# A two-layer decode kernel: wider copies in the chain's matmuls, another first head in the second layer, and finer V transfers

## The chip, the cores and the metric

The kernel runs on one core of a Trainium2 chip. The metric is the device time of one execution in microseconds (us), and lower is better. A core has a matrix engine (TensorE: PE for its matmuls, PEld for its weight loads), VectorE (DVE), ScalarE (ACT), GpSimd (POOL) and SyncE (SP), which here issues every transfer. Transfers run on 16 DMA engines. Matmul results land in PSUM, which has eight banks of 512 fp32 columns; everything else lies in SBUF.

## The reference

Two layers run one after the other with the same weights and the same caches. Each is an attention block with cached keys and values, and then an MLP block. B = 8 rows (batch), one new token each, D = 448, 16 query heads on 8 cached heads, 4096 cached positions, head size 256, all bf16.

```python
def A(x, k_cache, v_cache, wq, wo):      # x: [8, 1, 448], caches: [8, 8, 4096, 256]
    q = (x @ wq) in 16 heads of 256      # two query heads to a cached head
    p = softmax(q @ k.T * 256 ** -0.5)   # over 4096 positions
    return (p @ v) @ wo
def B_(x, w1, w2, w3, w4):
    h = gelu(layernorm(x) @ w1)          # shifted along S by pads; S = 1, so the shifts leave zeros
    x1 = x + shifted(h) @ w2
    return x1 + gelu(layernorm(x1) @ w3) @ w4
x = x + A(layernorm(x)); x = x + B_(layernorm(x))    # layer 1
x = x + A(layernorm(x)); x = x + B_(layernorm(x))    # layer 2
```

With S = 1 every shifted part is zero, so the w1 and w2 products drop out. What stays is attention, projection, and the w3/w4 MLP. Nearly all bytes are the caches: a head of K or V of one row is 2 MB, or four *quarters* of 512 KB.

## The kernel before, in words

**Slots.** SBUF has 30 slots of one quarter (`kv`). A row needs its K and V in both layers. To read less, some quarters stay in SBUF from the first layer to the second: K of the five *kept* heads 3 to 7 (`KEEP_K`), and six quarters of V (`KEEP_V`: all of head 7, quarters 2 and 3 of head 6). K must be transposed on the way (four fp32 transposes into a bank `psT`, L1145, then a copy back by DVE, L1129, or ACT, L1130). The last two quarters of head 7's K (`HOLD`) don't go back to SBUF at first: they stay transposed in the four `psT` banks until the second layer. Then their place is made by scoring head 7's quarters 0 and 1, after which the banks are copied into those slots (`back_in` in `front`). Heads 0 to 2 are the *free* heads; nothing of them is kept.

**Stages of a row.** `front` takes one head's scores: 16 matmuls a quarter with the cached keys as weights and the query as the moving operand, copied 24 times over two columns, 48 columns in all (L972), then the softmax. `back` does the PV product (8 matmuls a quarter, L1033), sums the four partition groups (L1057) and multiplies by `wo` (L1082). After the eighth head of layer 1 comes what is called the *chain* here: the turn of the summed projection row into columns (10 matmuls) and the last head's projection (20), both on L914 and L917; the norm's sums (L710); 56 matmuls with w3 (L818); gelu; 70 matmuls with w4 (L914, L917, `y_mm`); and the second layer's queries, 16 matmuls a head (L802). All of these have one useful column. It is copied along the moving operand: 24 times for queries and w3 (`QW`, `HW`), 12 times for w4, the turn and the projection (`YW`). Results of the chain and the scores share one PSUM bank, `psM`: scores from column 256 on, the chain's from `SC` = 448 and `YC` = 451 on.

**Order.** The program is written as a list of operations with priorities (`Plan.op`). A planner (`Plan.schedule`) runs them through a model of the engines with fixed durations and puts each engine's instructions in a fixed order; the chip then waits by semaphores, but never reorders. The planner does three things that matter here.
- Loads have a fixed order (`prio=loads[0]`), and SP is in order. `next_kv` joins up to four neighbouring quarters of one head into one transfer if as many neighbouring slots are free. A slot is free when the last PV or score on its old content is done.
- Where PE would idle over 0.1 us, it puts in `filler` matmuls (L1344) as long as the columns in the last 3.413 us are under `TARGET` = 3500. For an operation of the chain it counts 20 columns a matmul, whatever its real width (`pe`).
- The chain's operations have priority over all others (`CH`).

The order of heads in the second layer comes from `MIX` and `l2_heads`: 7, 6, 5, 4, 3, then the free ones 0, 1, 2. While a row's chain runs, the next row's free heads 0 to 2 have their scores already; their `back`, 12 quarters of V, is what the DMA loads then. After these come V of the second layer: head 6 (two quarters), 5, 4, then K of head 0, and so on. `mid` runs the chain's MLP and the queries of the first `QFIRST` heads (`QLAST` in the last row); `fronts_of` takes the queries of the other heads, one head ahead.

Of the kernel before, what the change touches and what calls it, by code (L numbers as in the profile page):

```python
# [8 lines left out]
D = 448  # L9
HKV = 8  # L10
DH = 256
F = 1792
NC5 = 5
# [8 lines left out]
KEEP_V = 6  # L22
# [5 lines left out]
OUT_AT = 23.5  # L28
QLAST = 1
BACKS = (0, 3, 6)  # L30
# [3 lines left out]
PV1 = PV0 + DH  # L34
QW, HW, YW = 24, 24, 12
SC = 448
YC = 451

# [20 lines left out]
class Unit:  # L59

    def __init__(self, tile, u, keep):
        self.tile, self.u, self.keep, self.slot = tile, u, keep, None


class Plan:
# [67 lines left out]
    def schedule(self):  # L135
# [30 lines left out]
        n = 0  # L166
# [14 lines left out]
        def next_kv(i):  # L181

            u = sp_next[i].unit
            m = 1
            while m < 4 and i + m < len(sp_next) and sp_next[i + m].unit is not None and \
                    sp_next[i + m].unit.tile is u.tile and sp_next[i + m].unit.u == u.u + m and \
                    sp_next[i + m].unit.keep == u.keep:
                m += 1  # L190
            late = max(free["sp"], dma_end - self.LEAD)
            times = sorted(set(x for x in self.free_at if x < 1e9))
            if not times:
                return None
            for t in [max(free["sp"], times[0])] + [x for x in times if free["sp"] < x <= late]:
                fit = [(k, a) for k, a in runs(t) if k >= m]
                if fit:
                    break
            else:
                t = max(late, times[0])  # L200
                m = min(m, max(k for k, a in runs(t)))
                fit = [(k, a) for k, a in runs(t) if k >= m]

            before = sp_next[i - 1].unit if i else None
            if before is not None and before.tile is u.tile:
                for k, a in fit:
                    if a <= before.slot + 1 <= a + k - m:
                        return t, m, before.slot + 1
            k = min(k for k, a in fit)
            fit = [a for k2, a in fit if k2 == k]  # L210
            q = min(fit) if u.keep else max(fit) + k - m
            return t, m, q
# [235 lines left out]
def bass_interleave_layers__gqa_block_cached__mixer_s_mlp__decode_kernel(  # L448
# [160 lines left out]

    def load(cache, b, h, units, keep=()):  # L610

        out = {}
        tile = (cache, b, h)
        for u in units:
            x = out[u] = Unit(tile, u, u in keep)
            o = plan.op("sp", None, 0.0, "kv", wr=[("s", x, 0), ("s", x, 1)], prio=loads[0])
            o.unit = x
            loads[0] += 1
        return out
# [45 lines left out]

    CH = -10 ** 6
    urge = [CH]

# [4 lines left out]

    def pe(fn, n, rd=(), wr=(), banks=(), name="chain", prio=None, pairs=None):
        if prio is None:
            prio = urge[0] + len(plan.ops)
        d = 0.06 + 0.026 * n
        return plan.op("pe", fn, (d, d, 20 * n, pairs or n), name, rd=rd, wr=wr, banks=banks, prio=prio)

# [145 lines left out]
    def column_sums():  # L825

        def one(kc):
            return mask[:, kc:kc + 1]
        for g in range(4):
            pe(lambda t, g=g: q_mms(t, range(8 * g, 8 * g + 8), one, psM, SC, 1, QW), 32,  # L830
               rd=["mask"] + WQ, wr=["psM"], banks=[M], prio=len(plan.ops))

            dv(lambda v, g=g: v.tensor_copy(
                cs_q[:, 8 * g:8 * g + 8].rearrange("p (h c j) -> p h c j", c=2, j=2),
                psM[:, SC:SC + 8].rearrange("p (h j c) -> p h c j", c=2, j=2)),
               rd=["psM"], wr=["cs_q"], banks=[M], prio=len(plan.ops))

    def column_sums_h():
        def one(kc):
            return mask[:, kc:kc + 1]  # L840
        pe(lambda t: h_mms(t, one, psM, SC, 1, HW), 56, rd=["mask"] + W3, wr=["psM"], banks=[M],
           prio=len(plan.ops))
        dv(lambda v: v.tensor_copy(cs_h[:, :], psM[:, SC:SC + 14]), rd=["psM"], wr=["cs_h"], banks=[M],
           prio=len(plan.ops))
# [3 lines left out]
    def mlp(src, skey, n, dst, dkeys):  # L848

        few = n < 3  # L850
        ch, kb, bk = (psM[:, SC:], "psM", M) if few else where[0]
        yw, yc = (YW, YC - SC) if few else (n, 0)
        m = 14 * n
        h_, a_, b_ = hb[:, 0:m], g1[:, 0:m], g2[:, 0:m]
        if few:

            sums(src, skey, n)
            moments(True, n)

            for r in range(n):  # L860
                dv(lambda v, r=r: v.tensor_scalar(t_h[:, r * 14:(r + 1) * 14], cs_h[:, :], minus_mean(n, r),
                                                  rsy[:, 1, r:r + 1], ALU.mult, ALU.mult),
                   rd=["mom", "rsy", "cs_h"], wr=["t_h"] if r == 0 else [("t_h", r)])
            pe(lambda t: h_mms(t, lambda kc: src[:, kc, 0:n], ch, 0, n, HW if n == 1 else 12), 56,
               rd=[skey] + W3, wr=[kb], banks=[bk])
            for r in range(n):
                dv(lambda v, r=r: v.scalar_tensor_tensor(
                    hb[:, r:m:n], ch[:, r:m:n], rsy[:, 1, r:r + 1], t_h[:, 14 * r:14 * r + 14],
                    ALU.mult, ALU.add), rd=[kb, "rsy", "t_h"] + [("t_h", r)] * (r > 0),
                   wr=["hb"] if r == 0 else [("hb", r)], banks=[bk])  # L870
        else:
            norm(src, skey, True, n)
            pe(lambda t: h_mms(t, lambda kc: yb[:, kc, 0:n], ch, 0, n, n), 56,
               rd=YB + W3, wr=[kb], banks=[bk])
            dv(lambda v: v.tensor_copy(h_, ch[:, 0:m]), rd=[kb], wr=["hb"], banks=[bk])
# [20 lines left out]
        def y_mm(t):  # L896
# [6 lines left out]
            return last  # L903
        pe(y_mm, 70, rd=["hT"] + W4, wr=[kb], banks=[bk])
        ps4 = ch[:, yc:yc + NC5 * yw].rearrange("p (a n) -> p a n", n=yw)[:, :, 0:n]
# [20 lines left out]
    KEPT_K[HKV - 1] = range(4 - HOLD)  # L926
    KEPT_V = {HKV - 1: range(max(4 - KEEP_V, 0), 4), HKV - 2: range(min(8 - KEEP_V, 4), 4)}
    done = {}

    def front(layer, b, h):  # L930

# [25 lines left out]
        for u in range(4):  # L957
# [6 lines left out]
            def sc(t, u=u, q=ks[u]):  # L964
                last = None
                for s in range(8):
# [9 lines left out]
                    rd=qk + [("s", ks[u], 0), ("s", ks[u], 1)],  # L976
                    wr=[("sc", par, x) for x in range(u, 4)], banks=[bk])
            if u in back_in:
# [34 lines left out]
    def back(layer, b, h):  # L1013
# [10 lines left out]
        fresh_v = [u for u in range(4) if u not in vs]  # L1024
        vs.update(load(A_v_cache, b, h, fresh_v, keep_v))
        for u in range(4):
# [62 lines left out]
        if k == HKV - 1:  # L1089
# [5 lines left out]
            def turn(t):  # L1095
# [6 lines left out]
            pe(turn, 10, rd=["hb", "g1", "g2", "hT", "selR"], wr=["psM"], banks=[M], name="turn",  # L1102
               prio=hi)
            dv(lambda v: v.tensor_tensor(acc[layer][:, :], xin, psM[:, YC:YC + NC5 * YW:YW], ALU.add),
               rd=["psM", xk], wr=[ak], banks=[M], name="acc", prio=hi)
        if k == HKV:
            def wo_mm(t):
# [6 lines left out]
                return last  # L1114
            pe(wo_mm, 20, rd=[("oT", no), "wo0"], wr=["psM"], banks=[M], name="wo", prio=hi)
            dv(lambda v: v.tensor_tensor(xout, acc[layer][:, :], psM[:, YC:YC + NC5 * YW:YW], ALU.add),
# [17 lines left out]
    def transpose_piece(i, pc, hold):  # L1134

        while tcount[0] % NT in held_banks:
            tcount[0] += 1
# [39 lines left out]
    def mid(b, heads):  # L1177

        src = x2c[b % 2]
        mlp(x1c[b % 2], ("x1", b), 1, src[:, :, 0:1], [("x2", b)])  # L1180
        sums(src, ("x2", b), 1, SC + 32)
        second_queries(b, heads[0], None, lambda: dv(
            lambda v: v.tensor_single_scalar(mom2[b % 2][:, :], psM[:, SC + 32:SC + 35], 1.0 / D, ALU.mult),
            rd=["psM"], wr=[("mom2", b)], banks=[M]))
# [12 lines left out]
    def second_queries(b, h, prio, then=lambda: None):  # L1197

        q, src = q2T[b % 2], x2c[b % 2]
        pe(lambda t: q_mms(t, range(4 * h, 4 * h + 4), lambda kc: src[:, kc, 0:1], psM, SC,  # L1200
                           1, QW), 16, rd=[("x2", b)] + WQ, wr=["psM"], banks=[M], prio=prio)
        then()
# [30 lines left out]
    def first_queries():  # L1233
# [14 lines left out]
        for c in range(2):  # L1248
# [3 lines left out]
               dur=0.3, rd=["psM"], wr=[("q1T", c)], banks=[M])  # L1252

    free_heads = list(range(HKV - KEEP_K))
    kept_heads = list(range(HKV - KEEP_K, HKV))
    l2_heads = kept_heads[::-1]

    q_todo = {}

    def fronts_of(layer, b, h):  # L1260
        if layer:

            todo = q_todo[b]
            for h2 in [x for x in todo if x == h] + [x for x in todo if x != h][:1]:
                second_queries(b, h2, len(plan.ops))
                todo.remove(h2)
        front(layer, b, h)

# [4 lines left out]
    def both(layer, b, heads, ahead=(), lag=1):  # L1273
# [4 lines left out]
        for i in range(n + lag):  # L1278
            if i < n:
                tasks.append(("f", layer, b, heads[i]))  # L1280
            tasks += [("f",) + a for a, at in zip(ahead, AT[3 - len(ahead):]) if at == i - n]
            if i >= lag:
# [30 lines left out]
    for b in range(B):  # L1313
# [3 lines left out]
        mid(b, order2[:first])  # L1317
        q_todo[b] = order2[first:]
        if b < B - 1:
            run([("b", 0, b + 1, h) for h in free_heads])  # L1320
# [82 lines left out]
```

## Time and profile before

| | |
|---|---|
| time, median of 4 runs | 1111.84 us (1109.38 to 1116.4) |
| the profiled execution's own time | 1114.11 us |
| its span, first to last instruction | 1112.0 us |
| PE, PEld, DVE, ACT, POOL busy | 87%, 70%, 51%, 26%, 9% |
| mean granted clock of TensorE | 0.931 |
| bytes moved, mean rate | 441.13 MB, 397 GB/s |
| transfers of V | 137 of 512 KB, 49 of 1024, 3 of 1536, 55 of 2048 |
| time from issue to landing (median) | 7.6 us for 512 KB, 16.6 us for 2048 KB |

The profile is one execution. Its span is cut into 40 slices, with busy shares, the clock that TensorE was granted, and the rate of the DMA. Other views list instructions in order of time, who waited for whom, and sums over chosen stretches. A matmul's time is partly modelled, so a busy PE isn't PE at its peak.

### The profile page before, as it was taken

Reading aid. Unit: us, or ns where it says so; the run is one execution under the profiler, and the core shown is the slowest. Engines: PE = TensorE matmul, PEld = TensorE weight load, DVE = VectorE, ACT = ScalarE, POOL = GpSimd, SP = SyncE. Lnnn points to the kernel's source line nnn. Section 1 sums busy time; section 2 is a strip of 40 time slices with the busy share of each in tenths; the row PEclk is TensorE's granted clock in tenths of the full one; section 3 lists DMA queues with packets and bytes.
Section 4 is the critical chain, followed back from the end, with each engine's and each line's share of the span. In section 5 each row is a group of like instructions: output and inputs, shape, how many; then the busy total and the mean of one; then the engine's idle time right before and its main releaser. Section 6 shows DMA issues by size and latency. Waiting matters only on the chain.

```text
span 1112.0 us, 42670 instructions
## 1 busy us (share of the span) xinstructions
PE 965.2 (87%) x19528; PEld 778.9 (70%) x19528; DVE 570.4 (51%) x1784; ACT 286.2 (26%) x841; POOL 97.6 (9%) x275
## 2 busy tenths in 40 slices
PE   5899889897889988898888897988879898898987
PEld 4678657785668756697577775778557785696674
DVE  4345445564455553565445554555445665365544
ACT  1133113340223312243123321233112331233120
POOL 0000010010100101011010100100010000111010
PEclk9899999997999988899899998999899998899897
DMA  9999999999999999999999999999999999999893
GB/s 335 409 425 419 390 403 423 425 416 374 395 426 425 393 340 421 423 426 416 351 423 425 421 378 371 423 423 422 394 384 425 424 399 363 413 424 415 322 419 167
DMA packets 56115, 441.13 MB, mean 397 GB/s; under 512 B 6000, under 2 KB 9216, under 8 KB 28800
## 3 DMA queue, kind: packets, MB, share of 16 engines
q1 hardware_dynamic: 55936, 438.41, 97.0%
q8 instruction: 153, 2.51, 0.9%
q14 instruction: 26, 0.21, 0.0%
HBM read 438.38 MB, written 0.01 MB: 394 GB/s over the span
## 4 chain that ended last, share of the span: by engine, by line
PE 54%; DMA 36%; DVE 5%; issue 3%; SPq 1%; ACT 0%; POOL 0%
DMA kv<-in_A_k_cache_dram 24%; PE psT L1145 20%; PE psM L972 15%; DMA kv<-in_A_v_cache_dram 11%; PE psP L1033 8%; PE psR L1082 3%; PE psM L802 2%; PE psM L914 1%; PE psM L917 1%; DVE oS L1047 1%; PE psP L1057 1%; DVE oS L1049 1%; PE psM L818 1%; SPq L604 1%; PE psP L1344 1%
## 5 line engine op out<-in xcount | busy, mean ns | idle before, releaser
L1145 PE MATMUL psT<-ident_f,kv 128*128 128x128 f32 x2816 | 393.0, 285 | 28.3 <-DMA kv<-in_A_k_cache_dram 25.1
L1129 DVE COPY kv<-psT 128x512 f32<-128x512 f32 x418 | 286.8, 690 | 176.1 <-PE psT L1145 173.2
L1145 PEld LDWEIGHTS psT<-ident_f,kv 128*128 128x128 f32 x2816 | 315.8, 145 | 51.7 <-DMA kv<-in_A_k_cache_dram 31.9
L1130 ACT COPY kv<-psT 128x512 f32<-128x512 f32 x318 | 185.1, 586 | 465.6 <-PE psT L1145 393.8
L1033 PE MATMUL psP<-kv,pT 128*2 128x256 bf16 x4096 | 175.1, 289 | 30.7 <-DMA kv<-in_A_v_cache_dram 16.4
L972 PEld LDWEIGHTS psM<-q2T,kv 128*128 128x128 bf16 x4096 | 124.0, 98 | 49.6 <-issue 40.3
L972 PE MATMUL psM<-q2T,kv 128*128 128x48 bf16 x4096 | 138.8, 186 | 17.4 <-issue 14.7
L972 PEld LDWEIGHTS psM<-q1T,kv 128*128 128x128 bf16 x4096 | 135.8, 97 | 17.7 <-issue 10.9
L972 PE MATMUL psM<-q1T,kv 128*128 128x48 bf16 x4096 | 144.7, 184 | 1.4 <-issue 1.0
L1033 PEld LDWEIGHTS psP<-kv,pT 128*2 128x2 bf16 x4096 | 80.9, 84 | 65.1 <-DMA kv<-in_A_v_cache_dram 21.3
L993 POOL PARTITION_ALL_REDUCE gm<-pm x128 | 45.4, 355 | 753.8 <-DVE pm L991 750.6
L988 DVE COPY sS<-psM 128x64 f32<-128x64 f32 x128 | 28.6, 223 | 132.9 <-PE psM L972 129.5
L1003 ACT ACTIVATE pT<-sS,nb,fac 128x32 bf16<-128x32 f32 x128 | 52.7, 418 | 162.5 <-DVE nb L997 162.5
L1047 DVE CAST oS<-psP 128x256 bf16<-128x256 f32 x128 | 54.0, 422 | 49.6 <-PE psP L1033 47.0
L1082 PE MATMUL psR<-wo_sb,oT 128*1 128x448 bf16 x448 | 68.1, 388 | 7.1 <-DVE oT L1063 3.6
L1007 POOL PARTITION_ALL_REDUCE Db<-rs x128 | 51.0, 398 | 225.3 <-ACT pT L1003 225.3
L1057 PEld LDWEIGHTS psP<-sel,oS 128*128 128x128 bf16 x512 | 25.6, 99 | 52.4 <-DVE oS L1049 46.2
L1057 PE MATMUL psP<-sel,oS 128*128 128x2 bf16 x512 | 32.2, 166 | 33.1 <-DVE oS L1049 32.4
L1003 ACT ACTIVATE pT<-sS,nb 128x32 bf16<-128x32 f32 x128 | 40.9, 326 | 74.3 <-DVE nb L997 74.3
L1049 DVE TENSOR_TENSOR oS<-psP,oS 128x256 bf16<-128x256 f32 x128 | 54.1, 423 | 3.1
L802 PE MATMUL psM<-x2c,wq_sb 128*128 128x24 bf16 x768 | 36.4, 184 | 4.5 <-issue 2.2
L802 PEld LDWEIGHTS psM<-x2c,wq_sb 128*128 128x128 bf16 x768 | 30.2, 98 | 14.2 <-issue 5.6
(156 smaller groups left out, 580.6 us busy)
## 6 DMA issues: line engine op xcount, KB each, us to landing
kv<-in_A_k_cache_dram SPq DMA_DIRECT2D x66, 2048.0 KB, 20.0
kv<-in_A_v_cache_dram SPq DMA_DIRECT2D x55, 2048.0 KB, 16.6
kv<-in_A_v_cache_dram SPq DMA_DIRECT2D x137, 512.0 KB, 7.6
kv<-in_A_v_cache_dram SPq DMA_DIRECT2D x49, 1024.0 KB, 11.1
kv<-in_A_k_cache_dram SPq DMA_DIRECT2D x32, 1024.0 KB, 11.9
kv<-in_A_k_cache_dram SPq DMA_DIRECT2D x4, 1536.0 KB, 11.7
kv<-in_A_k_cache_dram SPq DMA_DIRECT2D x12, 512.0 KB, 7.9
kv<-in_A_v_cache_dram SPq DMA_DIRECT2D x3, 1536.0 KB, 8.3
```

Source lines behind the costliest of these rows:

```text
L802: last = t.matmul(bank[:, at + i * step:at + i * step + copies], w, r, start=(kc == 0), stop=(kc == 3))
L972: last = t.matmul(ps[:, SB + 2 * i:SB + 2 * i + 2 * REP], a[:, c:256:2], bcast(rhs(c), REP, 1), start=(c == 0), stop=(c == 1))
L1003: return a.activation(pT[nr][:, :, :].rearrange("p i j -> p j i")[:, jj, :], sview[:, jj, :], ACT.Exp, bias=nb[nm][:, jj:jj + 1], scale=sc ...
L1007: plan.op("pool", lambda gp: gp.partition_all_reduce(Db[nr][:, :], rs[nr][:, :], P, RO.add), 0.5, "sum", rd=[("rs", nr, 0), ("rs", nr, 1)] ...
L1033: last = t.matmul(ps[g4:g4 + 2, PV0:PV0 + DH], pT[nr][:, i, :], slot_ap(q, s * 256, 256), start=(i < 4), stop=(i >= 28), skip_group_check= ...
L1047: plan.op("dve", lambda v: v.tensor_copy(oS[:, 0, :], po), 0.36, "o", rd=[("pv", par, x) for x in range(4)], wr=["oS0"], banks=[bk], prio=hi)
L1049: plan.op("dve", lambda v: v.tensor_tensor(oS[:, 1, :], po, oS[:, 0, :], ALU.subtract), 0.36, "o", rd=["oS0"] + [("pv", par, x) for x in r ...
L1057: last = t.matmul(ps[:, PV1 + 2 * c:PV1 + 2 * c + 2], oS[:, w, c:DH:2], sel[:, :], start=(w == 0), stop=(w == 1))
L1082: last = t.matmul(psR[r:r + 1, 0:D], oT[no][:, i % 2, i // 2:i // 2 + 1], wo_sb[:, a:a + D], start=(k == 1 and i < 2), stop=(k == HKV - 1 ...
L1129: return e.tensor_copy(dst, psT[bank][:, :])
L1130: return e.copy(dst, psT[bank][:, :])
L1145: last = t.transpose(psT[bank][:, s * P:(s + 1) * P], src, ident_f[:, :])
```

## The change

The matmuls of the chain get 48 copies of their one column instead of 24 or 12 (36 columns' worth for the first MLP product of the last two rows, which has two useful columns). The w4, turn and projection results move to columns 0 to 239 of `psM`, which are zeroed once; the second norm's sums move from `SC` + 32 to `SC` + 56. The planner now counts the chain's real widths, and a longer duration for it where it believes the clock to be low.

The second layer's order of kept heads becomes 6, 7, 5, 4, 3. All four quarters of head 6's K are in SBUF. The queries of a further head follow a `front` instead of going ahead of it, and in the last row the chain takes the queries of two heads.

V of the free heads of every row but the first, in layer 1, is loaded one quarter a transfer.

```diff
-QLAST = 1
+QLAST = 2
+QAFTER = 1
+BOOST = None
+L2 = (3, 4, 2, 1, 0)
+MOST = 1
+MOST2 = 4
-QW, HW, YW = 24, 24, 12
+QW, HW, YW = 48, 48, 48
-YC = 451
+YC = 0
...
-            while m < 4 and i + m < len(sp_next) and sp_next[i + m].unit is not None and \
+            while m < u.most and i + m < len(sp_next) and sp_next[i + m].unit is not None and \
...
-    def pe(fn, n, rd=(), wr=(), banks=(), name="chain", prio=None, pairs=None):
+    def pe(fn, n, rd=(), wr=(), banks=(), name="chain", prio=None, width=20):
         d = 0.06 + 0.026 * n
-        return plan.op("pe", fn, (d, d, 20 * n, pairs or n), name, rd=rd, wr=wr, banks=banks, prio=prio)
+        return plan.op("pe", fn, (d, max(d, 0.06 + n * width / 1200), width * n, n), name, ...)
...
-            pe(lambda t: h_mms(t, lambda kc: src[:, kc, 0:n], ch, 0, n, HW if n == 1 else 12), 56,
+            pe(lambda t: h_mms(t, lambda kc: src[:, kc, 0:n], ch, at, n, HW if n == 1 else 36), 56,
...
-        pe(y_mm, 70, rd=["hT"] + W4, wr=[kb], banks=[bk])
+        pe(y_mm, 70, rd=["hT"] + W4, wr=[kb], banks=[bk], width=yw)
...
-        vs.update(load(A_v_cache, b, h, fresh_v, keep_v))
+        most = MOST if (layer == 0 and b and h in free_heads) else MOST2 if h == l2_heads[1] and layer else 4
+        vs.update(load(A_v_cache, b, h, fresh_v, keep_v, most))
...
-        sums(src, ("x2", b), 1, SC + 32)
+        sums(src, ("x2", b), 1, SC + 56)
...
+        dv(lambda v: v.memset(psM[:, 0:NC5 * YW], 0.0), dur=0.3, rd=[("q1T", 0), ("q1T", 1)],
+           wr=["psM"], banks=[M])
...
-    l2_heads = kept_heads[::-1]
+    l2_heads = [kept_heads[i] for i in L2]
...
     def fronts_of(layer, b, h):
-        if layer:
-            todo = q_todo[b]
-            for h2 in [x for x in todo if x == h] + [x for x in todo if x != h][:1]:
-                second_queries(b, h2, len(plan.ops))
-                todo.remove(h2)
-        front(layer, b, h)
+        if not layer:
+            return front(layer, b, h)
+        todo = q_todo[b]
+        if h in todo:
+            todo.remove(h)
+            second_queries(b, h, len(plan.ops))
+        if not QAFTER and todo:
+            second_queries(b, todo.pop(0), len(plan.ops))
+        front(layer, b, h, BOOST if h == first2[b] else None)
+        if QAFTER and todo:
+            second_queries(b, todo.pop(0), len(plan.ops))
```

`BOOST` = None and `MOST2` = 4 leave priorities and sizes as they are.

## The prediction

> **What bounds the kernel now.** I read the page first: engines, transfer rates, chain.
>
> ```profile
> PE 965.2 (87%) x19528; PEld 778.9 (70%) x19528; DVE 570.4 (51%) x1784; ACT 286.2 (26%) x841; POOL 97.6 (9%) x275
> GB/s 335 409 425 419 390 403 423 425 416 374 395 426 425 393 340 421 423 426 416 351 423 425 421 378 371 423 423 422 394 384 425 424 399 363 413 424 415 322 419 167
> DMA packets 56115, 441.13 MB, mean 397 GB/s; under 512 B 6000, under 2 KB 9216, under 8 KB 28800
> PE 54%; DMA 36%; DVE 5%; issue 3%; SPq 1%; ACT 0%; POOL 0%
> ```
>
> The rate sits at 420 to 426 GB/s and dips eight times. 441.13 MB at 424 GB/s would take 1040 us, so 72 of the 1112 us are not streaming. The last quarter of V lands at 1097.5 us, so 14.5 us are the tail; about 7 us are the start (22.3 MB moved by 60 us). The rest are the dips. Next, the stretches view: two stretches between dips, then 27 us around each dip. Columns: stretch, length, busy time of PE, PEld, DVE, ACT, POOL, then granted clock, DMA share, GB/s.
>
> ```profile
> 170.00:245.00 75.00, 68.70 (x1242) 59.98 (x1235) 44.17 (x108) 27.14 (x74) 6.78 (x18) 0.98 1.00 423
> 707.00:780.00 73.00, 66.63 (x1228) 57.73 (x1226) 42.14 (x103) 25.28 (x68) 6.77 (x18) 0.98 1.01 423
> ```
> ```profile
> 126.00:153.00 27.00, 23.33 (x580) 16.27 (x581) 12.57 (x60) 3.10 (x11) 1.51 (x4) 0.94 1.01 392
> 259.00:286.00 27.00, 21.54 (x520) 14.51 (x523) 12.08 (x58) 2.29 (x7) 0.75 (x2) 0.75 0.95 349
> 393.00:420.00 27.00, 21.55 (x522) 14.76 (x525) 12.15 (x58) 2.19 (x7) 0.75 (x2) 0.80 0.92 337
> 527.00:554.00 27.00, 22.60 (x560) 15.64 (x561) 13.09 (x61) 3.20 (x11) 1.38 (x4) 0.87 0.95 351
> 660.00:687.00 27.00, 22.95 (x560) 16.02 (x558) 13.46 (x61) 2.30 (x7) 1.11 (x3) 0.87 0.96 354
> 792.00:819.00 27.00, 23.35 (x550) 15.85 (x551) 11.95 (x59) 2.30 (x7) 1.11 (x3) 0.81 0.97 359
> 926.00:953.00 27.00, 22.89 (x583) 15.91 (x582) 14.22 (x65) 3.10 (x11) 1.36 (x4) 0.87 0.96 360
> 1027.00:1054.00 27.00, 24.10 (x519) 17.70 (x518) 15.68 (x64) 4.42 (x13) 1.11 (x3) 0.81 0.89 322
> ```
>
> A dip's loss is 27 - 27 x rate/424: 2.0, 4.8, 5.5, 4.6, 4.5, 4.1, 4.1, 6.5, together 36 us. That pot is what the change can reach. Each dip is a row's chain (out projection, MLP, queries). Why it starves the DMA shows in the timeline of the fifth dip (start, length, engine, line):
>
> ```profile
> 670.51 1.27 PE L914 MATMUL psM<-hT,w_sb 128*128 128x12 bf16 x42
> 671.72 1.45 PE L917 MATMUL psM<-hT,w_sb 128*64 128x12 bf16 x28
> 673.10 0.60 PE L1033 MATMUL psP<-kv,pT 128*2 128x256 bf16 x8
> ...
> 676.44 0.80 PE L972 MATMUL psM<-q2T,kv 128*128 128x48 bf16 x16
> 677.28 0.59 ACT L1130 COPY kv<-psT 128x512 f32<-128x512 f32 x1 [7.26 <-PE psM L972]
> 677.53 0.68 DVE L1129 COPY kv<-psT 128x512 f32<-128x512 f32 x1
> ...
> 678.77 0.97 PE L972 MATMUL psM<-q2T,kv 128*128 128x48 bf16 x32
> ```
>
> At a chain 18 K and 6 V quarters are kept, so 6 of the 30 slots circulate. A V quarter landed at 669.62; its PV matmuls stood behind the second MLP product and ran at 673.10; only then did SP issue into that slot (673.74). Twelve V quarters of the next row's free heads go round like this, then V of heads 6, 5, 4. A full round of 6 quarters lasts 6 x 1.25 = 7.5 us and an issue needs 4.0 us at least to land, so 3.5 us of delay on PE are free and the rest is lost.
>
> **48 copies.** Added columns per chain: 56 x 24 = 1344 (first product), 70 x 36 = 2520 (second), 20 x 36 + 10 x 36 = 1080 (projection and turn), 16 x 24 = 384 for each head's queries. Their own time at full clock is nothing: 16 matmuls of 48 columns (L972) take 0.57 us, some 25 ns apart, no more than 16 of 24 columns (L802, 0.61). At half clock the 48-column ones take 0.80, 40 ns apart, while L802 keeps its 0.61 (673.74 to 674.35 us).
>
> What they buy is clock. I added up matmul columns in windows of 3.41 us (the length of the shortest half-clock spell in the clock records; fp32 counted twice, PV a quarter, since four run side by side). Of 29 windows under 2500 columns, 28 are followed by half clock; of 24 between 2500 and 3000, 12; of 259 above, 1. The second dip's windows hold 1836, 1816, 1536, 1820; the third's 2580, 2600, 1064, 2548. Some 5,700 added columns lift most of these over 3000. Against that stand fillers (L1344, 248 columns), which the planner places up to a target of 3500 and will place less often: 102 in the eight stretches, 3,200 columns a dip. Net at least +2,500. Half clock in the stretches is 2 x 27 x (1 - clock), together 69 us; I expect 25, so 44 less. Price: loss against half-clock time over the eight dips gives 0.28 us per us; without the first, where weights still land, 0.13. So 6 to 12 us; I take 8, nearer the lower slope, since the chain's own latency does not shrink. A ceiling: PV of a quarter takes 0.60 against 0.39 us, scores 0.80 against 0.57, some five such pieces a window, 13 windows, 13 us. The floor is below zero: see the last rival.
>
> The Trainium skill (TensorE: Matmul & The Clock Gate, HAM oscillation) gives as the rule that PE must have no idle gap above about 3.4 us. The longest PE idle in the fifth stretch is 1.57 us, yet its clock is 0.87. By the rule alone there would be nothing to win here and this term would be 0; the rows decide against it.
>
> **Head 6 first.** Head 7's quarters 2 and 3 lie in the transpose banks; after its first score two evictions (0.59 and 0.68 us) must pass, and its four scores last 3.35 us on average from first to last over the eight rows, freeing two slots; head 6's four slots follow until 6 to 9 us. Head 6 first: 64 scores at 27 ns are 1.8 us, four slots by about 2.3 us, head 7's two some 3 us later; and only one head's queries stand before the first score (16 matmuls, 0.55 us less). So V of heads 5 and 4 is issued 1 to 2 us earlier. It pays only where landings after the first score are starved: 0.9 to 1.8 us in the second and fifth dip, under 0.5 in others. Between 0 and 8 us in all, I take 4. Two queries in the last row's chain and the later query of the next head: 16 matmuls moved, hidden by PV, 0 (0.5 us if uncovered). The 240-column memset: 0.27 us by the 256-column row, once, under the first loads.
>
> **Single quarters.** The sizes of the free heads' V issues show 18 of two or three quarters in the seven later rows, the rest single already. So SP gets about 20 more issues at 0.4 us, hidden by its slot waits. A pair is freed by its second landing; single, its first quarter is reissued 1.25 us earlier. Starved landings next to such pairs add up to 5 us in dips four to seven. But the second dip, single but for one pair, lost 4.8 us, no less than the others. Queued singles land 1.27 us apart, pairs and quads 1.23 to 1.25: 38 quarters x 0.03 = 1 us. Between +1 and -5; I take -1.
>
> The Trainium skill (DMA: Bandwidth & Descriptors, Measured) says to batch to 1 MiB or more, at about 2 us fixed per transfer. An estimate by it, unoverlapped, would be 20 x 2 = 40 us lost; the landings 1.27 us apart show the fixed part overlapped.
>
> **Tail.** From the last landing to the end 14.5 us, half clock from 1101.9 on. The second product waits for hT, then at most 0.2 us for a filler. 36 and 48 copies at half clock would cost 98 x 14 ns = 1.4 us, a full clock saves 0.3. I take 0.
>
> Sum: -8 - 4 - 1 = -13 us. The profiled execution took 1114.11 us (span 1112.0 and 2.1 around it), 2.3 above the median 1111.84; carried over: 1099.
>
> **The rivals.** (1) *No change:* the planner takes out fillers as copies come in, and PV stays behind the chain in PE's fixed order. For it: the 3500 target, and waits like 669.62 to 673.10, which are order, not clock. Against: three fillers only in the second dip. The clock gives 0, the order its 4: 1108. (2) *Slower:* head 6 first makes the first PV of the layer need loaded quarters (V of head 6, 0 and 1), where head 7's needed none. Quarter 1 landed 0.5 to 3.6 us after the first score in five of seven rows; PV is due about 5 us after it (1.8 for the scores, 2.9 from the score copy to the sum, as at 680.74 to 683.64). If PE reaches it before the landing, everything behind waits and head 7's four V slots stay shut. It decides once quarter 1 lands over 5 us after the first score; 3 us more in seven rows is 21, less the 8 of the clock: 1125. For it: the first and third dip (8.2 and 5.9 us); against: the five others. Half clock that stayed would add to it at most 1.8 us a dip. (3) The change could fail to keep the clock and still free slots early; that lies in (1).
>
> **How the numbers follow.** Forecast 0.62, no change 0.20, slower 0.18. Half a percent, 5.6 us, is about what a measurement can tell. Low end: 12 + 8 + 5 = 25 less, 1087. High end: past the no-change case into the slower one, 1118; what is left out is most of the slower case above that and a little below the low end.
>
> **What would show it.** Right: clock above 0.93 in the eight stretches, rate above 365, fewer fillers, first score followed by 64 scores without an eviction between, no V transfer of a free head above 512 KB. Wrong: clock up and rate unchanged (order is the cause); clock unchanged (fillers gave it back); PE idle before L1033 on V of head 6 (rival 2).

## The result, and the profile after

The changed kernel takes 1116.99 us (median of 41 runs, 1109.18 to 1125.59) against 1111.32 for the kernel before (62 runs): a ratio of 1.0056, with an interval of 1.0044 to 1.0069. By the ratio it is 6.2 us slower; the two medians are 5.7 apart. The forecast was 1099, faster. The profiled execution took 1120.65 us (span 1118.8), which is 3.7 above its own median, so what follows reads places and shapes from the profiles, and takes what a change is worth from medians and ratios.

The page of the changed kernel:

```profile
PE 985.8 (88%) x19493; PEld 802.2 (72%) x19493; DVE 576.1 (51%) x1783; ACT 287.8 (26%) x843; POOL 97.6 (9%) x275
GB/s 336 409 424 421 388 398 425 424 419 345 415 423 427 398 331 421 424 422 415 341 425 424 422 401 362 424 426 416 359 407 423 426 384 368 415 420 409 296 396 162
DMA packets 58851, 441.13 MB, mean 394 GB/s; under 512 B 6304, under 2 KB 9520, under 8 KB 33840
PE 61%; DMA 26%; DVE 6%; issue 4%; SPq 1%; ACT 1%; POOL 0%
```

PE is busy 20.6 us longer with 35 fewer matmuls, and its share of the chain that ended last rises from 54% to 61%, while the share of the DMA falls from 36% to 26%. Between dips the rate is what it was.

The same eight stretches, 27 us around each dip (busy times, then granted clock, DMA share, GB/s):

```profile
126.00:153.00 27.00, 24.83 (x586) 18.13 (x584) 12.55 (x60) 3.10 (x11) 1.51 (x4) 1.00 1.00 385
260.00:287.00 27.00, 23.94 (x533) 17.61 (x534) 12.43 (x58) 2.07 (x7) 1.11 (x3) 0.81 0.90 338
396.00:423.00 27.00, 21.57 (x518) 15.91 (x518) 12.50 (x56) 2.14 (x7) 0.75 (x2) 1.00 0.95 336
528.00:555.00 27.00, 24.15 (x538) 17.21 (x539) 12.43 (x60) 2.07 (x7) 0.79 (x3) 0.87 0.94 343
661.00:688.00 27.00, 22.76 (x526) 16.70 (x527) 11.85 (x57) 2.07 (x7) 0.89 (x3) 0.94 0.95 345
793.00:820.00 27.00, 23.82 (x525) 17.09 (x523) 12.46 (x58) 2.14 (x7) 0.75 (x2) 0.81 0.94 345
929.00:956.00 27.00, 23.86 (x539) 17.80 (x539) 13.04 (x61) 2.10 (x8) 1.11 (x3) 0.88 0.97 359
1033.00:1060.00 27.00, 24.26 (x496) 19.74 (x497) 14.33 (x63) 4.04 (x13) 1.24 (x4) 0.87 0.82 292
```

The clock rose: half clock here, 2 x 27 x (1 - clock), is 44 us, down from 69. Yet the loss against 424 GB/s grew from 36 to 41 us. The third stretch shows it best: clock 1.00 instead of 0.80, rate 336 instead of 337. So the clock did come up and the rate did not follow it.

The timeline of the fifth dip (start, length, engine, line):

```profile
672.89 2.03 PE L921 MATMUL psM<-hT,w_sb 128*128 128x48 bf16 x42 [0.64 <-DVE hT L900]
674.85 1.28 PE L924 MATMUL psM<-hT,w_sb 128*64 128x48 bf16 x28
676.05 0.61 PE L1042 MATMUL psP<-kv,pT 128*2 128x256 bf16 x16
...
678.07 0.57 PE L979 MATMUL psM<-q2T,kv 128*128 128x48 bf16 x16
...
679.49 1.50 PE L979 MATMUL psM<-q2T,kv 128*128 128x48 bf16 x48
```

Two things are to be seen. The 64 scores of head 6 run without an eviction between, as the change says. And the 42 matmuls with w4 take 2.03 us where they took 1.27, although they have no more columns (48) than the scores below, of which 48 take 1.50. A matmul's record is about 0.18 us long in a pipeline, so the starts are (2.03 - 0.18) / 41 = 45 ns apart in the one row and (1.50 - 0.18) / 47 = 28 in the other. The groups, with shapes kept apart (count, then busy us and mean ns of one); the first row is the w3 product of the kernel before, the others are of the changed kernel:

```profile
L818 PE MATMUL psM<-x1c,w_sb 128*128 128x24 bf16 x336 | 13.0, 184 | 0.0
L808 PE MATMUL psM<-x2c,wq_sb 128*128 128x48 bf16 x768 | 53.2, 206 | 2.9 <-issue 1.5 <-DVE sS L996 1.2
L824 PE MATMUL psM<-x1c,w_sb 128*128 128x48 bf16 x336 | 20.6, 206 | 0.3 <-DVE mom L732 0.3
L921 PE MATMUL psM<-hT,w_sb 128*128 128x48 bf16 x378 | 17.5, 203 | 2.3 <-DVE hT L900 2.3
L979 PE MATMUL psM<-q1T,kv 128*128 128x48 bf16 x4096 | 144.1, 184 | 1.4 <-issue 0.9 <-DVE sS L996 0.3
```

The four rows of the changed kernel have the same tile and 48 columns. The matmuls of the three chain rows last 19 to 22 ns longer than those of the scores. What differs besides the weights is the moving operand: scores copy *two neighbouring* columns 24 times, the chain copies *one* column 48 times.

### The profile page after: what moved, and what is told of

The parts are those of the page before. It is cut to its first block, busy times and chain, and to the rows that moved or that the text cites. A ratio compares the mean times of both kernels' runs of the same rounds, so it can differ in the third digit from the quotient of the medians.

```text
span 1118.8 us, 42614 instructions
## 1 busy us (share of the span) xinstructions
PE 985.8 (88%) x19493; PEld 802.2 (72%) x19493; DVE 576.1 (51%) x1783; ACT 287.8 (26%) x843; POOL 97.6 (9%) x275
## 4 chain that ended last, share of the span: by engine, by line
PE 61%; DMA 26%; DVE 6%; issue 4%; SPq 1%; ACT 1%; POOL 0%
PE psT L1155 21%; DMA kv<-in_A_k_cache_dram 17%; PE psM L979 15%; PE psP L1042 9%; DMA kv<-in_A_v_cache_dram 9%; PE psM L808 4%; PE psR L1091 3%; PE psM L921 3%; PE psM L824 2%; PE psM L924 2%; DVE oS L1058 1%; DVE oS L1056 1%; PE psP L1066 1%; SPq L610 1%; PE psP L1363 1%
## 5 line engine op out<-in xcount | busy, mean ns | idle before, releaser
L1155 PE MATMUL psT<-ident_f,kv 128*128 128x128 f32 x2816 | 386.7, 282 | 15.6 <-DMA kv<-in_A_k_cache_dram 15.3
L1155 PEld LDWEIGHTS psT<-ident_f,kv 128*128 128x128 f32 x2816 | 309.1, 143 | 43.8 <-issue 20.9
L1042 PE MATMUL psP<-kv,pT 128*2 128x256 bf16 x4096 | 178.9, 286 | 23.4 <-issue 13.2
L979 PE MATMUL psM<-q2T,kv 128*128 128x48 bf16 x4096 | 138.0, 185 | 20.6 <-issue 18.9
L1042 PEld LDWEIGHTS psP<-kv,pT 128*2 128x2 bf16 x4096 | 78.1, 83 | 60.0 <-issue 23.3
L1091 PE MATMUL psR<-wo_sb,oT 128*1 128x448 bf16 x448 | 63.0, 361 | 7.8 <-DVE oT L1072 4.3
L808 PE MATMUL psM<-x2c,wq_sb 128*128 128x48 bf16 x768 | 53.2, 206 | 2.9 <-issue 1.5
L808 PEld LDWEIGHTS psM<-x2c,wq_sb 128*128 128x128 bf16 x768 | 44.7, 99 | 15.3 <-DVE sS L996 7.4
## 6 DMA issues: line engine op xcount, KB each, us to landing
kv<-in_A_v_cache_dram SPq DMA_DIRECT2D x52, 2048.0 KB, 16.6
```

The source lines that it names most:

```text
L808: last = t.matmul(bank[:, at + i * step:at + i * step + copies], w, r, start=(kc == 0), stop=(kc == 3))
L979: last = t.matmul(ps[:, SB + 2 * i:SB + 2 * i + 2 * REP], a[:, c:256:2], bcast(rhs(c), REP, 1), start=(c == 0), stop=(c == 1))
L1042: last = t.matmul(ps[g4:g4 + 2, PV0:PV0 + DH], pT[nr][:, i, :], slot_ap(q, s * 256, 256), start=(i < 4), stop=(i >= 28), skip_group_check= ...
L1091: last = t.matmul(psR[r:r + 1, 0:D], oT[no][:, i % 2, i // 2:i // 2 + 1], wo_sb[:, a:a + D], start=(k == 1 and i < 2), stop=(k == HKV - 1 ...
L1155: last = t.transpose(psT[bank][:, s * P:(s + 1) * P], src, ident_f[:, :])
```

## The experiments

The expectations go by numbered theories. Theory 1: a moving operand that reads one column 48 times is slow in itself, and that eats what the clock brings. Theory 2: the single quarters cost the time. Theory 3: the new order of heads and queries costs it. Theory 4: the planner's numbers make another fixed order of instructions, and that costs it, either because a low count makes the planner believe in half clock (4a) or because any other order moves the time by some 0.5% (4b). *Pitch* there is the time from the start of one matmul to the start of the next. Ratios are to the kernel before, run on the same chip; the interval is 95%.

**Parts undone or alone.** `e1_copies_back`: the changed kernel with the old copies. `e2_only_copies`: old head order, joined transfers, 48 copies. `e3_only_order` and `e4_only_singles`: the order and queries alone, the single quarters alone, both with old copies and the planner's old count. `e5_only_account`: only the planner's real widths and durations. All kernels here are cut out of the changed one and keep its results at column 0 and the memset.

```diff
-QW, HW, YW = 48, 48, 48                    # e1, e3, e4, e5
+QW, HW, YW = 24, 24, 12
-L2 = (3, 4, 2, 1, 0)                       # e2, e4, e5: old order; QLAST 1, QAFTER 0
+L2 = (4, 3, 2, 1, 0)
-MOST = 1                                   # e2, e3, e5
+MOST = 4
-  (d, max(d, 0.06 + n * width / 1200), width * n, n)      # e3, e4
+  (d, d, 20 * n, n)
```

> The changed kernel with 24, 24, 12 copies again (results stay at column 0; the planner counts these real widths); order and single quarters stay new. Theory 1: pitch back to 27 ns, clock back to about 0.93, time 1107 to 1113, ratio 0.996 to 1.002. Theories 2 and 3: what is left of the change is the costly part, so 1115 to 1120, ratio 1.004 to 1.008.

Measured 1115.65 us, 1.0056 [1.0031, 1.0082].

> The kernel before with 48 copies alone (with their place in PSUM and the planner's real widths); head 7 first, transfers joined as before. Theory 1: pitch 45 ns, x1c to x2c about 9.5 us, slower than before: 1114 to 1121, ratio 1.003 to 1.009. Theories 2 and 3: no slower than before, 1105 to 1112, ratio 0.994 to 1.001, since the clock rises above 0.94.

Measured 1124.39, 1.0138 [1.0102, 1.0174].

> The kernel before with the new order alone (head 6 first, a further head's queries after a front, two heads' queries in the last chain); 24, 24, 12 copies at column 0, the planner's 20 columns a matmul, joined transfers. Theory 1: the order gains a little or nothing, 1106 to 1112, ratio 0.995 to 1.001. Theory 3 (PV of head 6 waits for its loads, or the last row suffers): 1114 to 1118, ratio 1.003 to 1.007. Theory 2: as theory 1.

Measured 1110.15, 0.9999 [0.9978, 1.002].

> The kernel before with single quarters for V of the later rows' free heads alone; 24, 24, 12 copies at column 0, the planner's 20 columns a matmul, head 7 first. With 24 copies the changed kernel stayed at a ratio of 1.0056 and the new order alone gave 0.9999, so single quarters or the planner's real widths cost 0.6% there. Theory 2 (single quarters cost it): 1.004 to 1.008, 1114 to 1119 us. Theory 4 (the planner's real widths give another order of PE, and that costs it): 0.997 to 1.002, 1107 to 1112 us.

Measured 1111.55, 1.0005 [0.9985, 1.0025].

> The kernel before with the planner's real widths alone (24, 24, 12 copies at column 0, head 7 first, joined transfers): nothing changes on the chip but the order of instructions and the fillers. Theory 2: 0.997 to 1.002, 1107 to 1112 us. Theory 4: 1.004 to 1.008, 1114 to 1119 us.

Measured 1115.75, 1.0053 [1.0029, 1.0077].

Against the kernel before, the copies alone cost 1.4%, more than any theory expected, and the head order and the single quarters alone nothing. But taking the copies out of the changed kernel gains almost nothing either (e1, 1.0056 as well), and e5, whose only other edit is in numbers that the planner uses, costs 0.5%. So these five differ from before in two things at once: what runs, and the fixed order that the planner makes of it. None of them can be read as the price of its edit; the runs with one order, below, can.

**The same 48 columns out of two.** `e6_pairs` is the changed kernel with the chain's column stored twice, side by side, so that 48 columns are 24 readings of two; the planner gets the same input and makes the same order. The edit, shortened and in part put in words:

```diff
-    x1c = [sb(f"x1c{i}", [P, NC5, 3], bf) for i in range(2)]     # x, 1, -1; x2c, oT, selR likewise
+    x1c = [sb(f"x1c{i}", [P, NC5, 4], bf) for i in range(2)]     # x, x, 1, -1
-                    r = bcast(r, copies, 1)                      # r: one column
+                    r = bcast(r, copies // r.ap[-1][1], 1)       # r: two columns
-    scalar_tensor_tensor(hT[:, 0:m], a_, 1.0, h_, ...)
+    scalar_tensor_tensor(hT as [P, 14, 2], a_ twice, 1.0, h_ twice, ...)
```

> The changed kernel, but the chain's column is stored twice side by side, so that the 48 copies are 24 reads of two neighbouring columns, as in the scores. The planner's input, and so every engine's order, is that of the changed kernel. Theory 1 (a single column read 48 times costs 45 ns a matmul, for 27 with 24 copies, at either clock, and this is what made the change slower): start to start falls from 45 to 25-27 ns, MLP from x1c to x2c from 9.5 us on the mean to 8.2-8.7, time 1105 to 1110 us, ratio to the kernel before 0.994 to 0.999. Theory 2 (the single quarters cost it) and theory 3 (the new order of heads and queries cost it): pitch falls too, but the time stays at 1115 to 1118, ratio 1.004 to 1.007.

Measured 1106.56, 0.9964 [0.994, 0.9988]: faster than both kernels, 0.9% below the changed one. Its groups, the lines that answer to L808, L824 and L921:

```profile
L810 PE MATMUL psM<-x2c,wq_sb 128*128 128x48 bf16 x768 | 37.4, 188 | 4.1 <-issue 2.7 <-DVE sS L1002 1.2
L826 PE MATMUL psM<-x1c,w_sb 128*128 128x48 bf16 x336 | 13.3, 187 | 0.3 <-DVE mom L734 0.3
L927 PE MATMUL psM<-hT,w_sb 128*128 128x48 bf16 x378 | 11.6, 186 | 2.6 <-DVE hT L904 2.6
```

Same tile, same 48 columns, same count, and a third less busy time: 62.3 us in these three rows against 91.3. Theory 1 holds. `e12_copies36` measures the size between, with one column and `QW, HW, YW = 36, 36, 36`:

> The changed kernel with 36 single copies: one look at the pitch. Theory 1, as a rate: 45 ns for 48 copies is 0.94 ns a copied column, so 36 cost 34 ns and 24 are at the floor of 25 to 27. If instead the cost is a step above some width, 36 cost 27 or 45.

One run: 1113.68, too few to judge the time. Its group of the w3 product lies between:

```profile
L824 PE MATMUL psM<-x1c,w_sb 128*128 128x36 bf16 x336 | 16.1, 196 | 0.2 <-DVE mom L732 0.2
```

Start to start of neighbouring matmuls, mean over a trace: the w3 product of the kernel before, of e12, of the changed kernel and of e6; the scores of the same kernels, which copy two columns, agree with the last row.

| moving operand | full clock, ns | half clock, ns |
|---|---|---|
| one column, 24 times | 27 | 27 |
| one column, 36 times | 34 | 34 |
| one column, 48 times | 44 | 44 to 45 |
| two columns, 24 times | 25 to 26 | 40 to 41 |

One column costs 0.92 to 0.94 ns a copy (44 / 48, 45 / 48, 34 / 36) whatever the granted clock; at 24 copies that is 22 to 23 ns, under the spacing of 25 to 27 that is seen anyway. The Trainium skill (TensorE: Matmul & The Clock Gate, "Wait — 56ns, not 53.3ns?") gives the spacing as N / 2.4 GHz plus about 2.5 ns warm, and as N / 1.2 GHz cold, with a floor of about 25 ns; worked out for 48 columns, an estimate, that is 22.5 (so 25) and 40 ns. The pair's row agrees with it; the single column's 44 ns at full clock does not, and there the measurement decides.

**What the pairs are worth with the other parts.** `e7_pairs_joined` is e6 with `MOST = 4`, `e8_pairs_alone` has the old head order too, `e11_pairs_count20` is e6 with the planner's old count and durations.

> The changed kernel with the chain's column stored twice (25 ns a matmul) and with joined transfers: what single quarters are worth where the pitch is mended. That kernel with single quarters had a ratio of 0.9964. Theory 2: faster than it by 0.4 to 0.6%, 0.990 to 0.993. Theory 4: within 0.2% of it, 0.994 to 0.998. My estimate of the prediction (singles gain 1 us): 0.997.

Measured 1108.97, 0.9986 [0.9961, 1.0011].

> The kernel before with 48 copies as pairs of a column stored twice, and the planner's widths for it; head 7 first, joined transfers. With single columns the same kernel had a ratio of 1.0138. Theory 1: start to start 25 ns for 45, some 170 matmuls a chain, 3 us a row off: ratio 0.990 to 0.998, 1100 to 1109 us, and against the kernel with the new order beside it the order's worth with a mended pitch, which I expect at 0 to 0.4%. Against theory 1: 1.008 or more.

Measured 1110.6, 1.0002 [0.998, 1.0025].

> The changed kernel with the column stored twice (ratio 0.9964) and the planner's old count of 20 columns a chain matmul. Theory 4a does not bear here, since both counts are far above the threshold or near it: 0.994 to 0.999. Theory 1 holds if start to start is 25 ns and the ratio is below 1.000 with this order too; theory 4b: within 0.5% of 0.9964.

Measured 1107.54, 0.9973 [0.9953, 0.9994].

From e8 to e7 (head order) and from e7 to e6 (single quarters) it goes down by 0.16 and 0.22%, each within the intervals, 4.2 us in all; each step also brings a new fixed order. Both e7 and e8 came out above what was expected (0.998 at most). The planner's count makes no difference that shows here (e6 against e11).

**How much the fixed order alone moves.** `e9_count16` and `e10_count24`: old copies, old heads, joined, and only the number of columns that the planner counts for a matmul of the chain differs.

```diff
-  (d, d, 20 * n, n)
+  (d, d, 16 * n, n)        # e10: 24 * n
```

> The kernel before (24, 24, 12 copies, results at column 0), with 16 columns a chain matmul in the planner's count in place of 20. Real widths alone (24 for queries and w3, 12 for w4, turn and projection) gave a ratio of 1.0053. Theory 4a (undercounting the w4 product makes the planner believe in half clock, and its order is worse for that): 16 undercounts too, 1.003 to 1.008. Theory 4b (any other order moves the time by some 0.5% either way): anything from 0.995 to 1.006, not ordered by the count.

Measured 1116.28, 1.0059 [1.0036, 1.0082].

> The same with 24 columns in the planner's count. Theory 4a: overcounts more than 20 does, so no slower than before, 0.995 to 1.001. Theory 4b: anything from 0.995 to 1.006.

Measured 1116.3, 1.0058 [1.0035, 1.0081].

The same kernel with the old count of 20 is e16 below, at 1.0090: a number that reaches the chip only through the order and the fillers takes 0.3% off, whether it is raised or lowered, with an interval of about 0.3% either way. That speaks for 4b; 4a expected e10 at 0.995 to 1.001. So copies must be judged with the order held fixed. Four more runs complete that: old heads and joined transfers with the planner's old count, and 48 single (`e13`), 48 in pairs (`e14`) or 24 and 12 single copies (`e16`); and the new order, planned as for 48, with 24 and 12 on the chip (`e15`). The traces bear out that each set of three is one order: the instructions of every engine follow each other alike but for records that overlap in time and the two extra copies at the start of the pair kernels, with 238 fillers in each of the old and 204 in each of the new. In the same way e2 and e8 above are one order, with 212.

```diff
-   16, rd=[("x2", b)] + WQ, wr=["psM"], banks=[M], prio=prio, width=QW)     # e15: the planner is told 48
+   16, rd=[("x2", b)] + WQ, wr=["psM"], banks=[M], prio=prio, width=48)
```

> 48 single copies, heads 7 first, joined transfers, and the planner's old 20 columns and durations, so that the order of instructions is that of 24 copies. Against 24 single copies in the same order: theory 1 (slow reading, 18 ns on some 170 matmuls a chain, 3 us a dip, less what the clock gives back) 0.5 to 1.5% slower. Theory 4b (only the order matters): the same within 0.2%.

> The same order with 48 copies as pairs. Against 24 single copies in the same order this is the clock's worth alone: my prediction's term was 8 us, 0.7% faster (0.5 to 1.1%). Theory 4b: the same within 0.2%.

> The changed kernel's order of instructions (planned for 48 copies), with 24, 24, 12 single copies on the chip. Theory 1: faster than the changed kernel (1.0056) by 0.4 to 1%, 0.996 to 1.002, and slower than the pairs in this order (0.9964) by what the clock is worth, 0 to 0.7%. Theory 4b: 1.004 to 1.008, since the order is that of the changed kernel.

> Control: the kernel before with the chain's results at column 0 and the memset for it, nothing else; the planner puts out another order for that one operation more. Theory 4b: anything from 0.995 to 1.006. Otherwise 1.000, within 0.2%, and then the counts of 16 and 24 did cost 0.6%.

Measured: e13 1127.72, e14 1115.64, e15 1111.71, e16 1119.37. With the changed kernel, e6, e2 and e8 they make this table of ratios, one fixed order a row:

| | one column, 24 and 12 | one column, 48 | two columns, 48 |
|---|---|---|---|
| old heads, joined | 1.0090 [1.0069, 1.011] | 1.0155 [1.0131, 1.0178] | 1.0052 [1.0033, 1.007] |
| new heads, single quarters | 1.0004 [0.9982, 1.0026] | 1.0056 [1.0044, 1.0069] | 0.9964 [0.994, 0.9988] |
| old heads, joined, planned for 48 | not run | 1.0138 [1.0102, 1.0174] | 1.0002 [0.998, 1.0025] |

The kernel e1 is e15 but for the numbers the planner is told, and stands at 1.0056 against 1.0004: half a percent for order alone. Along each row only the copies differ, and the rows say the same. 48 single copies in place of 24 and 12 cost 0.65 and 0.52%. 48 in pairs gain 0.38 and 0.40%, 4.3 us, with an interval of about 0.3% either way; the likely reading is the clock without the slow reading of one column, expected at 0.5 to 1.1%. Between pair and single lie 1.03, 0.92 and 1.36%, the slow reading alone, 10 to 15 us.

Three stretches of e15 and of e6, the second, third and fifth dip, show the clock's side. First e15, then e6:

```profile
260.00:287.00 27.00, 23.34 (x558) 15.75 (x556) 13.62 (x63) 2.66 (x10) 1.11 (x3) 0.81 0.97 366
394.00:421.00 27.00, 24.40 (x542) 15.57 (x530) 12.83 (x60) 2.79 (x10) 1.11 (x3) 0.68 1.00 374
661.00:688.00 27.00, 24.95 (x596) 17.04 (x594) 12.37 (x59) 3.89 (x15) 2.26 (x6) 0.75 1.01 390
```
```profile
260.00:287.00 27.00, 19.87 (x535) 13.50 (x535) 12.91 (x60) 2.18 (x7) 1.11 (x3) 1.00 0.96 359
394.00:421.00 27.00, 20.88 (x554) 14.52 (x550) 12.98 (x61) 2.31 (x8) 1.11 (x3) 0.94 0.99 372
661.00:688.00 27.00, 22.75 (x625) 16.67 (x620) 13.16 (x61) 3.89 (x15) 2.26 (x6) 0.94 1.02 395
```

The clock goes from 0.68 to 0.94 in the third dip, and the rate stays where it was, 374 and 372. Over all eight stretches half clock is 97 us in e15, 44 in the changed kernel and 19 in e6; the loss is 28, 41 and 28 us. So the dips do not show the 4.3 us that e6 gains on e15, and neither do these two executions as a whole: that of e15 took 1106.97 us, 4.7 below its own median, that of e6 1108.33. Where the gain lies stays open.

The slow reading does show in the dips. Counted from 5 us before the end of each `x1c` (the first norm's input, ready before w3) to 22 us after it, the loss is 41 us in the changed kernel and 30 in e6, 45 in e13 and 37 in e14, 45 in e2 and 31 in e8; the spans of these executions are 12, 9 and 16 us apart. What goes with it is the latency of the chain, here in the fifth dip of the changed kernel and of e6 (`x2c` is what the second layer's queries read):

```profile
666.44 0.17 DVE L1125 TENSOR_TENSOR x1c<-acc,psM 128x5 bf16<-128x5 f32 x1 [1.17 <-PE psM L924]
676.16 0.17 DVE L913 SCALAR_TENSOR_TENSOR x2c<-psM,base 128x5 bf16<-128x5 f32 x1 [3.33 <-PE psM L924]
```
```profile
659.80 0.17 DVE L1134 TENSOR_TENSOR x1c<-acc,psM 128x10 bf16<-128x10 f32 x1 [0.83 <-PE psM L930]
667.68 0.17 DVE L919 SCALAR_TENSOR_TENSOR x2c<-psM,base 128x10 bf16<-128x10 f32 x1 [2.68 <-PE psM L930]
```

From the end of `x1c` to the end of `x2c` the mean over the rows is 8.43 us in e15, 9.50 in the changed kernel and 8.08 in e6; in the old order (e16, e13, e14) it is 8.18, 9.22 and 8.08, and 9.48 and 8.33 in e2 and e8. Single against pair is 1.42, 1.14 and 1.15 us a row, times eight rows 11, 9 and 9 us, against the 10, 11 and 15 measured in the time. Within one order, then, the chain's latency seems to be passed on nearly whole, in the third pair with something more. Across orders it does not rank the kernels: the kernel before has 8.75 and e16 has 8.18, and e16 is the slower one.

**Where e16 loses.** Its loss in the dips is that of the kernel before, 36 us each, and its last quarter of V lands at 1097.9 us against 1097.5. But 18.8 us follow that landing instead of 14.5. PE in the tail, first of the kernel before, then of e16:

```profile
1096.51 0.54 PE L1082 MATMUL psR<-wo_sb,oT 128*1 128x448 bf16 x4
1097.54 1.04 PE L1033 MATMUL psP<-kv,pT 128*2 128x256 bf16 x32 [0.48 <-DMA kv<-in_A_v_cache_dram]
1101.17 0.34 PE L710 MATMUL psM<-xf 128*128 128x4 bf16 x8
```
```profile
1097.97 1.02 PE L1042 MATMUL psP<-kv,pT 128*2 128x256 bf16 x16 [3.30 <-DMA kv<-in_A_v_cache_dram]
1099.93 0.95 PE L1091 MATMUL psR<-wo_sb,oT 128*1 128x448 bf16 x4
1105.37 0.40 PE L716 MATMUL psM<-xf 128*128 128x4 bf16 x8
```

In e16 PE idles for 3.30 us before it starts on that quarter, with another head's `wo` product (L1091) still to come, which stood ahead of the landing before (L1082). It runs at half clock from 1095.6 us to the end, before only from 1101.9. The last norm's sums (L710, L716) start 7.4 us after the landing instead of 3.7. The two kernels that share the order do alike: e13 and e14 idle for 3.2 and 2.9 us there, enter the tail at half clock, and have tails of 17.8 and 17.7 us. All other kernels with column 0 and the memset enter it at full clock, and their tails run from 13.4 to 16.6.

## Why the prediction was wrong

**The step that failed** is the first sentence on the cost of the copies: "Their own time at full clock is nothing: 16 matmuls of 48 columns (L972) take 0.57 us, some 25 ns apart, no more than 16 of 24 columns (L802, 0.61)." The nearest row by size was taken, but it had another operand: L972 copies two columns, the chain one. Measured 44 to 45 ns instead of 27. A chain up to its first score has 10 + 20 + 56 + 70 + 16 matmuls; 172 x 18 ns is 3 us a row at most (less for the 64-wide halves, which are 37 ns apart at full clock instead of 30). In its place the runs showed a price of 0.9 to 1.4%, 10 to 15 us, for single columns against pairs. The same section noted that L972 was 40 ns apart at half clock and "L802 keeps its 0.61". That was no clear warning: at the 40 / 48 ns a column of L972, 24 columns would take 20 ns, under the spacing of 25 to 27 that is seen anyway. No row of the kernel before copies one column more than 24 times, so the term had no near row, and it was put at nothing without a range.

**The clock**, taken as -8 us: copies did raise the clock, but the price did not hold. Half clock went from 69 to 44 us, not to 25; in pairs, which keep the forecast's terms, it did go to 19. But taking away 78 us of half clock (97 to 19, e15 to e6) was worth 4.4 us (0.40%), 0.06 us per us, and not in the dips as far as the traces show, where slopes of 0.13 to 0.28 across dips were used. Presumably dips with much half clock lost much for other reasons too. The count of columns that sets the clock was right in kind: with the order fixed, more columns raised it. The first count of the losses was also loose: 72 us less 14.5 for the tail and 7 for the start leaves 50 to the dips, and the eight stretches hold 36. The other 14 lie between them, in the changed kernel 16.

**Head 6 first**, taken as -4: alone, nothing against the kernel before (0.9999). It does what was said: on the mean over the rows the 64th score starts 13.6 to 15.0 us after `x1c` in the kernels with the new heads (the changed one, e1, e3, e6, e7, e11, e15), 15.3 to 17.0 in those with the old (before, e2, e8, e13, e14, e16). But the 128th starts at 18.6 to 20.1 against 19.5 to 20.8, so less of the gain is left 64 scores later. **Single quarters**, taken as -1: alone 1.0005. Against e16, which differs from e3 only in heads and from e4 only in single quarters, both are 0.8 to 0.9% faster, but e16 has the long tail of its order, so that is no price of either. With pairs the two together gave 4.2 us, no more than a new order alone moves. What the two are worth by themselves was not found.

**What the prediction lacked** is the planner. The path from before to after, step by step: results at column 0 with the memset, old copies and heads (e16) +0.90%; new heads, single quarters and the planner's count (e15) -0.85%; copies (changed kernel) +0.52%. Together +6.2 us. The first two each bring a new fixed order, and either is larger than the copies. Column 0 and the memset are in e3, e4 and e15 as well, all within 0.05% of before; and in e16's trace 4.2 of the 4.7 us by which its span is longer lie in the tail, which only the three kernels of its order enter at half clock. So that part goes with the order and not with column 0. The medians are 8 to 10 us apart, more than was expected of e16 (1.006 at most), and the rest was not found in these executions. Nor was it found what makes e1 slower than e15.

**The rivals.** "No change": it was right that the clock would bring less than forecast, but not on the cause, and it had no cost to set against it. "Slower", through V of head 6: it did not happen. PE's idle time before PV that waits for V fell from 16.4 to 9.3 us over the span (before, then changed):

```profile
L1033 PE MATMUL psP<-kv,pT 128*2 128x256 bf16 x4096 | 175.1, 289 | 30.7 <-DMA kv<-in_A_v_cache_dram 16.4
L1042 PE MATMUL psP<-kv,pT 128*2 128x256 bf16 x4096 | 178.9, 286 | 23.4 <-issue 13.2 <-DMA kv<-in_A_v_cache_dram 9.3 <-ACT pT L1011 0.3
```

Slower came, by another mechanism; the price that was added to it, "at most 1.8 us a dip" for copies at half clock, was of the right size (1.1 to 1.4 us a row), but holds at either clock.

**The signs that were set out.** Clock above 0.93 in the eight stretches: 0.90. Rate above 365: 343. Fewer fillers: 239 to 204, right. 64 scores without an eviction, and V of free heads in 512 KB transfers only (168 such transfers instead of 137): right. "Clock up and rate unchanged (order is the cause)" came nearest, and its reading was wrong in the main: the matmuls' own time is what the copies cost, and the order moved the time beside it.

## What to carry to other kernels

A matmul's row prices another only if the moving operand has the same pattern of reads, not just the same size: look at what is copied, and where no row has the pattern, put a range on the term. If copies are wanted to keep the clock up, copy two neighbouring columns rather than one. In a kernel whose instruction order is planned, re-planning alone moved the time by 0.3 to 0.5% here, as much as the edits were worth, so an edit must be judged against a control with the same order.

## What the runs showed of the hardware

A single 2-byte column that the moving operand reads again and again goes at 0.92 to 0.94 ns a column (48 and 36 copies), at full and at half clock alike, while two neighbouring ones copied to the same 48 columns go at 25 to 26 ns a matmul at full clock and 40 to 41 at half. With pairs, half clock is felt; with single columns, it hardly is (44 and 44 to 45 ns). Whether it is the reading of the operand or something behind it was not separated.
